# Local attention and SiLU MLP on one core: second MLP steps laid out behind a pair of first ones, and the q copy put ahead of the reciprocal on VectorE

## The chip, the core and the metric

The kernel runs on one core of a Trainium2 chip. The metric is the device time of one execution in microseconds (us), taken as the median of the runs; lower is better. The core has TensorE (PE, with its weight loads listed as PEld), VectorE (DVE), ScalarE (ACT), GpSimd (POOL) and SyncE (SP), which work through their own instruction streams and wait for one another through semaphores.

## What is computed

The inputs are q, k and v of shape 8 x 8 x 576 x 64 (batch, heads, positions, width) and two weights of 512 x 2048 and 2048 x 512. All are float32. Cut to what matters:

```python
# attention, per batch and head; S = 576, D = 64, factor = 4
q_d, k_d, v_d = means of q, k, v over groups of 4 positions        # 144 positions
out_d   = softmax(q_d @ k_d.T / 8) @ v_d                            # then repeated 4 times
out_loc = softmax(where(|i - j| < 4, q @ k.T / 8, -1e9)) @ v        # a band of 7 positions
x = (repeat(out_d, 4) + out_loc), heads side by side                # 4608 tokens x 512
# MLP
h = x @ w_in                                                        # 4608 x 2048
out = (h * sigmoid(h)) @ w_out                                      # 4608 x 512
```

## The kernel before

The attention goes by pairs of heads: pair p (0 to 31) holds heads 2p and 2p+1, and four pairs make one batch element, that is 576 tokens of x and all its 512 columns (column block kc is pair 4b+kc). The MLP goes by blocks j (0 to 8) of 512 tokens. x is kept transposed in `xT`, a ring of 1536 tokens, so block j can start only when the pairs that make its tokens are done: block 2 needs pair 11, block 3 pair 15, block 4 pair 19, block 5 pair 23, block 6 pair 27, blocks 7 and 8 pair 31.

The work is written as units. A unit is a few instructions on one engine, with a name. The names used below, for pair p:

- On PE: `T` transposes q into PSUM bank `o0` and k into bank `pe_`; `S` makes the scores in bank pair `AB`; `Z` makes the sums of exponentials and `PV` the weighted values, both in `CD`; `VP` makes v's group sums (up to pair 13 only); `RB` spreads the reciprocals over the partitions (up to pair 9 only). From n = 10 on, one unit `V`n holds S of pair n, T of pair n+1, PV of pair n-2 and Z of pair n-1, in this order of instructions. `g1_j_f` is a first MLP step: four matmuls (kc = 0 to 3) that make 128 columns (f of 16) of h for block j, in one of the two banks of `HP`. `g2_j_tt_part` is a quarter of a second MLP step: four matmuls of the product of 128 tokens (tt of 4) with w_out, into bank `o0` (from the 23rd step on alternately `pe_` and `o0`).
- On VectorE: `eq` copies the transposed q out of `o0` (ScalarE does it for pairs below 12); `mk` and `mq` make the group sums of k and q; `r` is the reciprocal of the sums in `CD`; `m` multiplies `CD` by the spread reciprocals `Rb` into `xo`; `k` masks the exponentials; `s` is the second half of SiLU on one g1.
- On ScalarE: `ek` copies k out of `pe_`; `x` and `xd` are the exponentials; `t` is the tanh of one g1 (so a bank of `HP` is free after g1, t and s); `o` copies a finished g2 out of its bank. From pair 10 on its queue also issues `z`, which writes the reciprocals to DRAM, and two `b`, which read them back spread over the partitions into `Rb`.
- On GpSimd: `c` and `cw` cast q/k and v; `va` and `vb` make v's group sums from pair 14 on out of the load `vq`; `a` adds the two attention results into `xT`.
- SP's queue issues the loads (`lq`, `lk`, four `lv`, three `lvq` per pair, released by the exponential of an earlier pair) and the `out` stores.

The order on each engine is not written out. The program creates the units in one sequence, and `Plan.order` then lays them out by list scheduling: with the costs written in the code it takes, on the engine that can go first, the ready unit with the lowest priority number among the next few (14 on PE, 40 on ScalarE and VectorE). A unit's number is its place in the sequence unless `prio` gives another; `t` and `s` have -1, `o` has -3, `r` has -400000, `z` and `b` have -500000. A dictionary `FIRST` can hold a written-out order for an engine's first units; in the kernel before it is empty. The order so found is then run in that order by each engine, with waits only where data or buffers ask for them.

The sequence from n = 10 on is one loop: V, then RB, VP and new loads where there are any, then four g1 and one g2 in its four parts, mixed. When the pairs are done, the loop goes on with g1 and g2 alone.

Of the kernel before, what the change touches and what calls it, by code (L numbers as in the profile page):

```python
# [15 lines left out]
NPAIR = B_ * H_ // 2  # L16
# [145 lines left out]


FIRST = {
}

class Plan:
# [109 lines left out]
def bass_hourglass_attn__then__act_silu_kernel(  # L277
# [9 lines left out]
    with kctx:  # L287
        E = kctx.enter_context
        L = Plan()
        res = {}  # L290

        def R(name, psum=False):
            if name not in res:
                res[name] = Res(name, psum)
            return res[name]

        def sb(name, shape, dt, n=1):
            ts = [E(nc.sbuf_tensor(f"{name}{i}", shape, dt)) for i in range(n)]
            return ts if n > 1 else ts[0]
# [22 lines left out]
        zr = sb("zr", [128, 72], F32, 2)  # L322
# [30 lines left out]
        def one(eng, name, cost, fn, r=(), w=(), dma=None, prio=None, dcost=0.0):  # L353
            u = L.unit(eng, name, cost, prio, dcost)
            L.op(u, fn, r, w, dma)
            return u
# [4 lines left out]
        def copy(eng, e, out_, in_):  # L361
            return e.activation(out_, in_, AF.Copy) if eng == "ACT" else e.tensor_copy(out_, in_)
# [3 lines left out]
        def half(j):  # L366
            return slice(64 * j, 64 * j + 64)
# [95 lines left out]
        def dma(eng, name, out_, in_, w, sem, dcost, r=(), prio=None, cost=0.42):  # L463
            return one(eng, name, cost, lambda s: s.dma_start(out_, in_), r, w, sem, prio, dcost)  # L464
# [98 lines left out]

        def pe_T(u, p):
            a, b = p % NB, (p - 1) % NB
            for r in range(9):
                for j, h, x, t, n in ((0, 0, 0, o0, a), (0, 1, 1, pe_, a), (1, 1, 0, o0, a), (1, 0, 1, pe_, b)):
                    o = t[half(h), 0:288].bitcast(BF16)[:, 64 * r:64 * r + 64]  # L570
                    w = qkb[n][half(j), x, 64 * r:64 * r + 64]
                    L.op(u, lambda e, o=o, w=w, j=j: e.transpose(o, w, idn[half(j), :]),  # L572
                         [R("id"), R(f"qkb{n}{x}")], [rE if x else rF])

        def after_T(p):
            j = p % NT
            eng = "ACT" if p < NEQ else "DVE"
            one(eng, f"eq{p}", 0.68 if p < NEQ else 0.72, lambda e: copy(
                eng, e, qT[j][:, :].rearrange("p (g r) -> p g r", r=9),
                o0[:, 0:288].bitcast(BF16).rearrange("p (r g) -> p g r", r=9)),  # L580
                r=[rF], w=[R(f"qT{j}")])
            one("ACT", f"ek{p}", 0.68, lambda e: e.activation(  # L582
                kT[j][:, 3:579].rearrange("p (g r) -> p g r", r=9),
                pe_[:, 0:288].bitcast(BF16).rearrange("p (r g) -> p g r", r=9), AF.Copy),
                r=[rE], w=[R(f"kT{j}")])
            one("DVE", f"mk{p}", 0.74, lambda e: e.tensor_reduce(  # L586
                kd[j][:, 0:SD], kT[j][:, 3:579].rearrange("p (g r) -> p g r", r=4), AX.X, ALU.add),
                r=[R(f"kT{j}")], w=[R(f"kd{j}")])
            if p >= NMQ:
                one("DVE", f"mq{p}", 0.74, lambda e: e.tensor_reduce(  # L590
                    qd[j][:, :], qT[j][:, :].rearrange("p (g r) -> p g r", r=4), AX.X, ALU.add),
                    r=[R(f"qT{j}")], w=[R(f"qd{j}")])
                return
            half_ = vt[:, :, :].rearrange("p a b -> p (a b)")[:, 0:288].rearrange("p (g r) -> p g r", r=2)
            q4 = qT[j][:, :].rearrange("p (g r) -> p g r", r=4)
            u = L.unit("POOL", f"mq{p}", 1.2)
            L.op(u, lambda g: g.tensor_tensor(half_, q4[:, :, 0:2], q4[:, :, 2:4], ALU.add),
                 r=[R(f"qT{j}")], w=[R("vt")])
            L.op(u, lambda g: g.tensor_tensor(qd[j][:, :].unsqueeze(2), half_[:, :, 0:1], half_[:, :, 1:2], ALU.add),
                 r=[R("vt")], w=[R(f"qd{j}")])  # L600
# [49 lines left out]
        def acc(p):  # L650
            return (HP, rH) if p < 4 and p % 2 else (CD_, rCD_)
# [48 lines left out]
        def after_Z(p):  # L700
            i, u = p % 2, p % NR
            CD, rCD = acc(p)
            if p < NDIR:
                (h, m, l), rp = [rpart[p % 2][:, k, :] for k in range(3)], rpr[p % 2]
                zs, rest, rz = zr[i][:, :], rrest[p % 2][:, :], R(f"rrest{p % 2}")
                sg = [R("sgn0"), R("sgn1")]
                one("DVE", f"r{p}", 0.56, lambda e: e.reciprocal(zs, CD[:, 0, 360:432]), r=rCD[:1], w=[R(f"zr{i}")],  # L707
                    prio=-400000)
                one("ACT", f"rh{p}", 0.25, lambda e: e.activation(h, zs, AF.Copy), r=[R(f"zr{i}")], w=[rp[0]],
                    prio=-400000)  # L710
                one("DVE", f"rx{p}", 0.2, lambda e: e.scalar_tensor_tensor(  # L711
                    rest, h, sgn[:, 0:1], zs, ALU.mult, ALU.add), r=[R(f"zr{i}"), rp[0]] + sg, w=[rz], prio=-400000)
                one("DVE", f"rm{p}", 0.15, lambda e: e.tensor_copy(m, rest), r=[rz], w=[rp[1]], prio=-400000)
                one("DVE", f"rl{p}", 0.2, lambda e: e.scalar_tensor_tensor(  # L714
                    l, m, sgn[:, 1:2], rest, ALU.mult, ALU.add), r=[rz, rp[1]] + sg, w=[rp[2]], prio=-400000)
                return
            one("DVE", f"r{p}", 0.56, lambda e: e.reciprocal(zr[i][:, :], CD[:, 0, 360:432]),
                r=rCD[:1], w=[R(f"zr{i}")], prio=-400000)
            eng = "ACT"
            dma(eng, f"z{p}", scr[u][0:74, :], zr[i][0:74, :], [R(f"scr{u}")], f"scr{u}", 0.2, r=[R(f"zr{i}")], prio=-500000)  # L720
            for h in range(2):
                src = bass.AP(tensor=scr[u].tensor, offset=scr[u].offset + 64 * h * 72, ap=[[0, 64], [1, 720]])
                dma(eng, f"b{p}", Rb[u][half(h), :], src, [R(f"Rb{u}{h}")], f"Rb{u}{h}", 0.85,
                    r=[R(f"scr{u}")], prio=-500000)
# [49 lines left out]
        def g1(j, f):  # L774
            n = ng1[0]
            ng1[0] += 1
            hb, tb = n % 2, n % 2
            t0 = (512 * j) % XR
            u = L.unit("PE", f"g1_{j}_{f}", 0.934)
            for kc in range(4):  # L780
                mm(u, hps[hb], w_in_sb[:, kc, 128 * f:128 * f + 128], xT[:, kc, t0:t0 + 512].bitcast(F32R),
                   [R(f"w_in{f // 4}")] + xblk(kc, 512 * j, 512 * j + 512), [rH[hb]], start=(kc == 0), stop=(kc == 3))
            one("ACT", f"t{j}_{f}", 0.62, lambda e: e.activation(th[tb][:, :], hps[hb], AF.Tanh, scale=0.5),  # L783
                r=[rH[hb]], w=[R(f"th{tb}")], prio=-1)
            one("DVE", f"s{j}_{f}", 0.71, lambda e: e.scalar_tensor_tensor(  # L785
                gT[j % 2][:, f, :], th[tb][:, :], 1.0, hps[hb], ALU.add, ALU.mult),
                r=[rH[hb], R(f"th{tb}")], w=[R(f"g{j % 2}_{f}")], prio=-1)
# [19 lines left out]
        def T(p):  # L807
            made.add(("T", p))
            u = L.unit("PE", f"T{p}", 0.45 if p > 1 else 0.9)
            pe_T(u, p)  # L810
            after_T(p)

        def VP(p):
            u = L.unit("PE", f"VP{p}", 0.4 if p > 1 else 0.8)
            pe_VP(u, p)
            after_VP(p)
# [69 lines left out]
        def G1(n):  # L886
            for _ in range(n):
                if todo:
                    g1(*todo.pop(0))

        def G2(parts):
            j, tt = todo2[0]
            u = 4 * j + tt
            bank, rb = (o0, rF) if u < 22 or u % 2 else (pe_, rE)
            for p in parts:
                g2(j, tt, p, bank, rb)
            if parts[-1] == 3:
                todo2.pop(0)
# [20 lines left out]
        while todo or todo2:  # L919
            if n < NPAIR + 2:  # L920
                V(n)
                if n <= NDIR:
                    RB(n - 1)
                if n <= NVP:
                    VP(n - 1)
                feed()
            G1(1)
            G2((0,))
            G1(1)
            G2((1,))  # L930
            G1(1)
            G2((2, 3))
            G1(1)
            n += 1
        P = Prog()
        for u in L.order({"PE": 14, "ACT": 40, "DVE": 40, "POOL": 30, "SP": 40}, FIRST):
            plan_log.append((u.start, u.cost, u.eng, u.name))
# [35 lines left out]
```

The softmax here doesn't subtract the row's maximum and nothing guards it: scores larger than these inputs give would overflow.

## Time and profile before

| what | value |
|---|---|
| median of 3 runs | 357.08 us (356.82 to 357.63) |
| the profiled execution | 357.98 us, its span 356.2 us |
| mean granted TensorE clock | 0.986 |
| one g1, in a row of eight matmuls | 0.92 us |
| one g2 of 16 matmuls | 3.45 to 3.47 us |
| reciprocal (r), q copy (eq) on VectorE | 0.61 us, 0.70 us |
| m, k, mk, mq, s on VectorE | 0.90, 0.45, 0.73, 0.74, 0.69 us |
| tanh (t), copy of a g2 (o) on ScalarE | 0.60 us, 0.60 us |
| loads into vq, Rb: from issue to landing (median) | 5.2 us, 4.2 us |

The times of single instructions come from the one profiled execution, whose span of 356.2 us is 1.8 us less than its own time. The profile's rows show start, duration, engine, line, operation and `out<-in` by the program's names without buffer numbers, and, in square brackets, how long the engine had been idle and what ended that. A line such as L359 or L464 belongs to a helper that issues every matmul or every DMA, so rows are told apart by tile: `HP` is g1, `o<-w_out_bf` is g2, `AB` is S or RB, `CD` is PV and Z, `o<-idn` and `pe_<-idn` are T.

### The profile page before, as it was taken

The numbers are of one execution on the slowest core, as the hardware profiler recorded it, in microseconds if no ns is written. First come the engines' busy times: TensorE is split into PE (matmuls) and PEld (weight loads), VectorE is DVE, ScalarE is ACT, GpSimd is POOL, SyncE is SP. The second block draws the span as 40 slices with busy tenths as digits, with TensorE's granted clock in tenths as the row PEclk, the third lists the DMA queues.
The fourth block names the chain that finished last, engine by engine and source line by source line (L and its number), as shares of the span: only waits on it lengthen the run. The fifth ranks groups of instructions, "written<-read, shape, count | busy, mean of one in ns | idle before, by whom it ended". The sixth has DMA issues, their size and how long they took to land.

```text
span 356.2 us, 11025 instructions
## 1 busy us (share of the span) xinstructions
PE 327.2 (92%) x4742; PEld 212.7 (60%) x4742; DVE 228.1 (64%) x392; ACT 181.8 (51%) x326; POOL 156.8 (44%) x203
## 2 busy tenths in 40 slices
PE   1574599899999999999999999999999999999996
PEld 0453477666666666666666665666665666666642
DVE  7589889876667777777776766677754434343400
ACT  2766478766554555555555554555543343434321
POOL 7977874272374675664667367555111100000000
PEclk9998689999999999999999999999999999999999
DMA  8999999946878877778887987873222000110012
GB/s 230 248 264 243 302 297 219 220 131 179 235 193 237 223 225 223 221 201 226 233 227 193 229 240 206 194 182 107 65 111 77 31 29 29 51 39 29 31 59 88
DMA packets 73506, 60.28 MB, mean 169 GB/s; under 512 B 47986, under 2 KB 55794, under 8 KB 73458
## 3 DMA queue, kind: packets, MB, share of 16 engines
q1 hardware_dynamic: 63818, 44.27, 47.5%
q10 hardware_dynamic: 5416, 9.02, 8.7%
q0 software_dynamic: 4224, 6.29, 7.5%
q8 instruction: 37, 0.61, 0.7%
q14 instruction: 11, 0.09, 0.1%
HBM read 51.76 MB, written 9.91 MB: 173 GB/s over the span
## 4 chain that ended last, share of the span: by engine, by line
PE 79%; DVE 7%; DMA 4%; SPq 4%; ACT 3%; issue 2%; POOL 1%; POOLq 0%; ACTq 0%; DVEq 0%
PE HP L359 35%; PE o L359 25%; PE pe_ L359 8%; PE CD L359 5%; SPq L464 4%; PE AB L359 3%; DMA vq<-in_v_dram 3%; PE o L572 1%; DVE rrest L711 1%; DVE rp L714 1%; DMA vs<-in_v_dram 1%; DVE Pt L628 1%; DVE xo L745 1%; DVE zr L707 1%; DVE gT L785 1%
## 5 line engine op out<-in xcount | busy, mean ns | idle before, releaser
L785 DVE SCALAR_TENSOR_TENSOR gT<-th,HP 128x512 bf16<-128x512 f32 x144 | 96.6, 684 | 101.2 <-ACT th L783 100.8
L359 PE MATMUL HP<-xT,w_in_sb 128*128 128x512 f32 x576 | 160.0, 416 | 1.6 <-DVE gT L785 0.7
L783 ACT ACTIVATE th<-HP 128x512 f32<-128x512 f32 x144 | 86.2, 599 | 75.3 <-PE HP L359 73.4
L359 PEld LDWEIGHTS HP<-xT,w_in_sb 128*128 128x128 f32 x576 | 106.0, 189 | 28.9 <-DVE gT L785 1.3
L359 PE MATMUL o<-w_out_bf,gT 128*128 128x512 bf16 x464 | 107.0, 380 | 0.0
L359 PEld LDWEIGHTS o<-w_out_bf,gT 128*128 128x128 bf16 x464 | 42.6, 98 | 54.3 <-issue 8.6
L769 POOL TENSOR_TENSOR xT<-xo 128x576 fp32r<-128x576 f32 (+3 forms) x48 | 42.9, 907 | 44.5 <-DVE xo L745 44.5
L800 ACT ACTIVATE osb<-o 128x512 f32<-128x512 f32 x29 | 17.4, 599 | 60.4 <-PE o L359 60.3
L559 POOL TENSOR_TENSOR vt<-vq 128x512 f32<-128x512 f32 x18 | 23.0, 1278 | 56.0 <-DMA vq<-in_v_dram 55.9
L544 POOL CAST qkb<-qk 128x1152 bf16<-128x1152 f32 x30 | 36.8, 1226 | 6.9 <-PE pe_ L572 4.7
L745 DVE TENSOR_TENSOR xo<-CD,Rb 128x720 f32<-128x720 f32 x30 | 27.0, 899 | 1.0 <-ACT Rb L735 0.6
L554 POOL CAST vb<-vs 128x640 bf16<-128x640 f32 x30 | 22.1, 736 | 11.3 <-PE CD L359 5.6
L572 PE MATMUL o<-idn,qkb 64*64 64x64 bf16 x576 | 17.4, 202 | 9.9 <-DVE qkb L539 6.3
L359 PE MATMUL pe_<-w_out_bf,gT 128*128 128x512 bf16 x112 | 26.4, 380 | 0.0
L586 DVE TENSOR_REDUCE kd<-kT 128x144 bf16<-128x576 bf16 x32 | 23.3, 731 | 0.9 <-ACT kT L582 0.8
L582 ACT ACTIVATE kT<-pe_ 128x576 bf16<-128x576 bf16 x32 | 21.0, 655 | 1.9
L628 DVE TENSOR_TENSOR Pt<-Pt,mask_bf 128x576 bf16<-128x576 bf16 x32 | 20.7, 647 | 0.8 <-ACT Pt L624 0.8
L624 ACT ACTIVATE Pt<-AB 128x576 bf16<-128x576 f32 x32 | 20.7, 646 | 0.6 <-PE AB L359 0.4
L572 PEld LDWEIGHTS o<-idn,qkb 64*64 64x64 bf16 x576 | 13.9, 117 | 9.7 <-DVE qkb L539 6.3
L572 PE MATMUL pe_<-idn,qkb 64*64 64x64 bf16 x576 | 16.3, 202 | 2.0 <-DVE qkb L541 1.0
L359 PEld LDWEIGHTS pe_<-w_out_bf,gT 128*128 128x128 bf16 x112 | 10.0, 98 | 13.6 <-issue 3.2
L590 DVE TENSOR_REDUCE qd<-qT 128x144 bf16<-128x576 bf16 x24 | 17.8, 742 | 0.0
(79 smaller groups left out, 311.9 us busy)
## 6 DMA issues: line engine op xcount, KB each, us to landing
vs<-in_v_dram SPq DMA_DIRECT2D x126, 80.0 KB, 4.2
qk<-in_q_dram SPq DMA_DIRECT2D x32, 288.0 KB, 3.6
out_dram<-osb SPq DMA_DIRECT2D x36, 256.0 KB, 3.3
qk<-in_k_dram SPq DMA_DIRECT2D x30, 288.0 KB, 4.8
Rb<-scr ACTq DMA_DIRECT2D x44, 180.0 KB, 4.2
vq<-in_v_dram SPq DMA_DIRECT2D x18, 256.0 KB, 5.2
w_in_sb<-in_moe_w_in_dram POOLq DMA_DIRECT2D x4, 1024.0 KB, 10.6
w_out_bf<-in_moe_w_out_dram POOLq DMA_DIRECT2D x4, 512.0 KB, 11.2
```

The source lines that it names most:

```text
L359: L.op(u, lambda t: t.matmul(out_, lhsT, rhs, start=start, stop=stop, skip_group_check=True), r, w)
L544: one("POOL", f"c{p}", 1.15, lambda g: g.tensor_copy(qkb[j][:, :, :], qk[i][:, :, :]), r=[R(f"qk{i}0"), R(f"qk{i}1")], w=[R(f"qkb{j}0"), R ...
L554: one("POOL", f"cw{p}", 0.72, lambda g: g.tensor_copy(vb[m][:, :, :], vs[i][:, :, :]), r=rr, w=[R(f"vb{m}")])
L559: one("POOL", f"va{p}", 1.3, lambda g: g.tensor_tensor(vt[:, :, :], vq[i][:, :, 0:128], vq[i][:, :, 128:256], ALU.add), r=rr, w=[R("vt")])
L572: L.op(u, lambda e, o=o, w=w, j=j: e.transpose(o, w, idn[half(j), :]), [R("id"), R(f"qkb{n}{x}")], [rE if x else rF])
L582: one("ACT", f"ek{p}", 0.68, lambda e: e.activation(kT[j][:, 3:579].rearrange("p (g r) -> p g r", r=9), pe_[:, 0:288].bitcast(BF16).rearra ...
L586: one("DVE", f"mk{p}", 0.74, lambda e: e.tensor_reduce(kd[j][:, 0:SD], kT[j][:, 3:579].rearrange("p (g r) -> p g r", r=4), AX.X, ALU.add), ...
L628: one("DVE", f"k{p}", 0.46, lambda e: e.tensor_tensor(Pt[m][:, :, :], Pt[m][:, :, :], mask_bf[:, :].unsqueeze(1).to_broadcast([128, 2, 288 ...
L745: one("DVE", f"m{p}", 0.92, prio=-450000 if L.boost else None, r=rCD + [R(f"Rb{u}0"), R(f"Rb{u}1")], w=[R(f"xo{x}")], fn=lambda e: e.tenso ...
L769: one("POOL", f"a{p}", 0.15 + n * 0.0019, lambda g, dst=dst, in0=in0, in1=in1: g.tensor_tensor(dst, in0, in1, ALU.add), r=[R(f"xo{x}")], w ...
L783: one("ACT", f"t{j}_{f}", 0.62, lambda e: e.activation(th[tb][:, :], hps[hb], AF.Tanh, scale=0.5), r=[rH[hb]], w=[R(f"th{tb}")], prio=-1)
L785: one("DVE", f"s{j}_{f}", 0.71, lambda e: e.scalar_tensor_tensor(gT[j % 2][:, f, :], th[tb][:, :], 1.0, hps[hb], ALU.add, ALU.mult), r=[rH ...
```

## The change

It has three parts.

1. `FIRST` is filled: the order of the first units is written out for all five engines, up to the unit RB9 on PE, ev9 on ScalarE, mq11 on VectorE, the last piece of a8 on GpSimd, and the first DMA of lv13 on SP. From there on the planner goes by its rule again.
2. `eqi` records the place of each pair's `eq` unit. The reciprocal of pair p (p of 10 and more) no longer has priority -400000, but the place of eq of pair p+2 plus a half; both belong to the same V step. For pairs 30 and 31, which have no such eq, it is the unit's own place.
3. In the loop, the four g1 and the g2 are created in another sequence: part 0 of g2, two g1, parts 1 to 3, two g1.

```diff
 FIRST = {
+    "PE": """
+        T0 T1 S0 T2 S1 Z0 VP0 T3 Z1 RB0 PV0 VP1 S2 T4 PV1 RB1 Z2 VP2 S3 T5 PV2 Z3 RB2 VP3 S4 T6 PV3 RB3 Z4
...
+        g1_0_14 RB8 g1_0_15 g1_1_0 g1_1_1 V10 g1_1_2 g1_1_3 VP9 g2_0_0_0 g2_0_0_1 g2_0_0_2 RB9""",
...
 }
...
+        eqi = {}
+
...
             eng = "ACT" if p < NEQ else "DVE"
+            eqi[p] = len(L.units)
             one(eng, f"eq{p}", 0.68 if p < NEQ else 0.72, lambda e: copy(
...
             one("DVE", f"r{p}", 0.56, lambda e: e.reciprocal(zr[i][:, :], CD[:, 0, 360:432]),
-                r=rCD[:1], w=[R(f"zr{i}")], prio=-400000)
+                r=rCD[:1], w=[R(f"zr{i}")], prio=eqi[p + 2] + 0.5 if p + 2 < NPAIR else None)
...
                 feed()
-            G1(1)
             G2((0,))
-            G1(1)
-            G2((1,))
-            G1(1)
-            G2((2, 3))
-            G1(1)
+            G1(2)
+            G2((1, 2, 3))
+            G1(2)
             n += 1
```

More of the change, by code (lines that the diff above doesn't have):

```diff
@@ L164 @@
 FIRST = {
+    "PE": """
+        T0 T1 S0 T2 S1 Z0 VP0 T3 Z1 RB0 PV0 VP1 S2 T4 PV1 RB1 Z2 VP2 S3 T5 PV2 Z3 RB2 VP3 S4 T6 PV3 RB3 Z4
+        VP4 S5 T7 Z5 RB4 VP5 PV4 g1_0_0 g1_0_1 S6 T8 g1_0_2 g1_0_3 RB5 Z6 g1_0_4 S7 g1_0_5 PV5 VP6 g1_0_6
+        RB6 T9 Z7 g1_0_7 g1_0_8 S8 PV6 VP7 g1_0_9 g1_0_10 RB7 T10 Z8 g1_0_11 g1_0_12 S9 PV7 VP8 g1_0_13
+        g1_0_14 RB8 g1_0_15 g1_1_0 g1_1_1 V10 g1_1_2 g1_1_3 VP9 g2_0_0_0 g2_0_0_1 g2_0_0_2 RB9""",
+    "ACT": """
+        lkx lk0 ckx eq0 ek0 cw0 eq1 ek1 cw1 x0 xd0 eq2 ek2 x1 xd1 ev0 rh0 eq3 ek3 eb0 rh1 ev1 x2 xd2 eq4 ek4
+        eb1 rh2 ev2 x3 xd3 eq5 ek5 eb2 rh3 ev3 x4 xd4 eq6 ek6 eb3 rh4 ev4 x5 xd5 eq7 ek7 eb4 rh5 ev5 t0_0
+        t0_1 x6 xd6 eq8 t0_2 t0_3 eb5 ek8 rh6 t0_4 x7 xd7 t0_5 ev6 t0_6 eb6 eq9 ek9 rh7 t0_7 t0_8 x8 xd8 ev7
+        t0_9 t0_10 eb7 eq10 ek10 rh8 t0_11 t0_12 x9 xd9 ev8 t0_13 t0_14 eb8 t0_15 t1_0 t1_1 eq11 ek11 rh9
+        t1_2 t1_3 x10 xd10 ev9""",
@@ new lines @@
+    "DVE": """
+        const const.1 const.2 const.3 const.4 const.5 const.6 const.7 const.8 const.9 const.11 const.10
+        const.12 const.14 const.13 const.15 const.16 const.17 const.18 const.19 const.20 const.21 const.22
+        const.23 zero const.24 const.25 const.37 const.38 const.39 const.40 const.41 const.67 const.70
+        const.68 const.71 cq0 const.26 const.27 cq1 ck0 ck1 const.62 const.63 const.64 const.65 mk0 mk1 k0
+        mk2 r0 k1 rx0 rm0 rl0 r1 mk3 m0 rx1 rm1 rl1 k2 r2 mk4 rx2 m1 rm2 k3 rl2 r3 mk5 m2 rx3 rm3 rl3 k4 r4
+        mk6 rx4 m3 rm4 k5 rl4 r5 mk7 rx5 m4 rm5 rl5 s0_0 s0_1 k6 mq8 s0_2 r6 s0_3 mk8 rx6 s0_4 rm6 k7 rl6 m5
+        s0_5 s0_6 r7 mq9 mk9 rx7 s0_7 rm7 s0_8 rl7 k8 m6 s0_9 s0_10 r8 mq10 mk10 rx8 s0_11 rm8 s0_12 rl8 k9
+        m7 s0_13 s0_14 s0_15 s1_0 s1_1 r9 m8 mk11 rx9 s1_2 rm9 s1_3 rl9 mq11""",
@@ new lines @@
+    "POOL": """
+        const.28 const.31 const.29 const.32 const.30 const.33 const.34 const.35 const.36 const.66 const.69
+        const.42 const.43 const.44 const.45 const.46 const.47 const.48 const.49 const.50 const.51 const.52
+        const.53 const.54 const.55 const.56 const.57 const.58 const.59 const.60 const.61 mq0 c2 mq1 c3 mq2
+        cw2 c4 w0 cw3 mq3 c5 a0 cw4 mq4 w1 c6 a1 cw5 mq5 a2 w2 c7 cw6 mq6 a3 c8 cw7 w3 a4 mq7 c9 cw8 w4 c10
+        w5 a5 w6 cw9 w7 a6 a7 c11 cw10 c12 cw11 cw12 c13 a8 a8.1 a8.2""",
@@ L165 @@
+    "SP": """
+        lq0 lq1 lk1 lv0.1 lv0.2 lv0.3 lq2 lv0e lv0 lk2 lv1 lv1.1 lv1.2 lv1.3 lq3 lk3 lv2 lv2.1 lv2.2 lv2.3
+        lq4 lk4 lv3 lv3.1 lv3.2 lv3.3 lq5 lk5 lv4 lv4.1 lv4.2 lv4.3 lq6 lk6 lv5 lv5.1 lv5.2 lv5.3 lq7 lk7
+        lv6 lv6.1 lv6.2 lv6.3 lq8 lk8 lv7 lv7.1 lv7.2 lv7.3 lq9 lk9 lv8 lv8.1 lv8.2 lv8.3 lq10 lk10 lv9
+        lv9.1 lv9.2 lv9.3 lq11 lk11 lv10 lv10.1 lv10.2 lv10.3 lv11 lv11.1 lv11.2 lv11.3 lq12 lk12 lq13 lk13
+        lv12 lv12.1 lv12.2 lv12.3 lq14 lk14 lv13""",
 }
```

## The prediction

> **What bounds the kernel now.** I read the page's busy times and its 40 slices first.
>
> ```profile
> PE 327.2 (92%) x4742; PEld 212.7 (60%) x4742; DVE 228.1 (64%) x392; ACT 181.8 (51%) x326; POOL 156.8 (44%) x203
> PE   1574599899999999999999999999999999999996
> ```
>
> TensorE (PE) is the limit from about 46 us on. The table of stages (PE, PEld, DVE, ACT, POOL busy; clock; DMA share; GB/s) says how completely:
>
> ```profile
> 46.00:78.00 32.00, 30.12 (x595) 22.42 (x594) 27.17 (x50) 23.82 (x46) 17.03 (x20) 0.99 1.09 226
> 145.00:187.00 42.00, 42.00 (x686) 27.17 (x686) 32.43 (x50) 21.92 (x39) 24.97 (x26) 1.00 0.79 222
> 187.00:216.00 29.00, 28.33 (x509) 18.43 (x507) 20.09 (x33) 15.44 (x28) 17.22 (x23) 1.00 0.85 226
> 216.00:248.00 32.00, 32.00 (x471) 20.49 (x458) 24.56 (x39) 16.62 (x29) 18.96 (x19) 1.00 0.67 171
> 275.00:339.00 64.00, 64.00 (x287) 39.11 (x285) 25.27 (x37) 26.35 (x44) 1.22 (x1) 1.00 0.10 36
> ```
>
> Pair 10 begins the part that the change reaches (V11 ends at 85 us). From there PE is idle in one place only, 0.67 us between 187 and 216. A busy PE can still hide a stall, so I measured the rhythm too: each reciprocal of L717 starts as its V step ends, so the distance of two of them is one period. VectorE's timeline gives
>
> ```profile
> 103.43 0.61 DVE L717 RECIPROCAL zr<-CD 128x72 f32<-128x72 f32 x1
> 111.56 0.61 DVE L717 RECIPROCAL zr<-CD 128x72 f32<-128x72 f32 x1
> ...
> 120.59 0.61 DVE L717 RECIPROCAL zr<-CD 128x72 f32<-128x72 f32 x1
> 121.11 0.70 DVE L362 COPY qT<-o 128x576 bf16<-128x576 bf16 x1
> ...
> 129.21 0.61 DVE L717 RECIPROCAL zr<-CD 128x72 f32<-128x72 f32 x1
> ...
> 206.93 0.61 DVE L717 RECIPROCAL zr<-CD 128x72 f32<-128x72 f32 x1
> ...
> 216.53 0.61 DVE L717 RECIPROCAL zr<-CD 128x72 f32<-128x72 f32 x1
> ```
>
> A plain period is 8.62 us (120.59 to 129.21): V, two g1, four g2, two g1. Periods with a VP step are 9.04. Three others are short because they hold three g1, not four (8.13 with a VP from V13 to V14; 7.70 from V21 to V22, made up by 9.55 with five after it; 7.74 from V29 to V30). Only V25 to V26 is long without return: 216.53 - 206.93 = 9.60, a loss of about 0.97 us. PE's timeline shows its cause:
>
> ```profile
> 212.11 1.97 PE L359 MATMUL HP<-xT,w_in_sb 128*128 128x512 f32 x7
> 214.75 0.50 PE L359 MATMUL HP<-xT,w_in_sb 128*128 128x512 f32 x1 [0.67 <-POOL xT L769]
> ```
>
> The last of eight matmuls, g1_5_0's with kc=3, waits for a23. POOL has a23 queued behind va27, cw27, vb27 and c28, and va27 waited 3.17 us for its vq load. In the kernel before, g1_5_0 stands ahead of V26, so V26 waits with it.
>
> **The skill.** "PSUM — Partial Sum Buffer", section "PSUM bank collisions raise a hardware error", has a PSUM bank guarded as a whole against two engines. The trace agrees: T's first transposes into o0 start after the ACT copy has left it (copy 109.44 to 110.04, T at 110.47). The same page, "Engine vs sequencer instructions", calls the ScalarE and VectorE queues strict FIFO; agreeing, a tanh ready at about 126.7 waits at 127.36 behind two b issues. "VectorE: DVE Perf Modes", section "The DRAIN you can't avoid", says that an instruction waits until the pipe is empty: here the copy starts 0.52 after a reciprocal of 0.61, so the records overlap by 0.09, and swapping the two leaves their sum as it is.
>
> **Part 1, FIRST.** I compared these five lists with the order that the kernel before lays out: all are its first 82 (PE), 100 (ACT), 141 (DVE), 81 (POOL) and 83 (SP) names, without a difference. Nothing before V11 moves: cost 0.
>
> **Part 2, eq ahead of r, 20 pairs.** No instruction is added. eq (0.70) starts 0.52 earlier, r (0.61) some 0.7 later. What would gain is g2, which needs bank o0 from eq. But eq ends at 121.11 + 0.70 = 121.81 and g2 starts at 122.46, when the two g1 ahead of it are through: 0.65 us of slack already, so the gain is 0. What could lose is r's chain. z goes out behind a tanh, about 1.1 us later (121.23 to 122.34). It has a row of cover: the b loads of that pair are issued at 126.21, and z needs 2.9 us (112.20 to 115.16, where b waits for nothing else). In about half of the periods b now stands ahead of the o copy at r + 3.5 (132.70 for r15); I expect it behind o in all, at r + 5.6 as for r14. Rb then lands at about r + 5.6 + 0.55 + 4.2 (the page's median) = 10.4; m starts at r + 12.3 (132.85 for r14), and would start about 0.4 later, because tanh outputs now overtake mq on VectorE. Slack 1.9 or more, 0 even at the longest landing (6.2). Cost taken: 0; bounds: -0.1 to +0.1 per period at most if landing stays in its range. The mq and k that finish some 0.4 later are used 3 us later or more. Behind the b issues a first tanh starts 0.3 later, which V covers (V15's period has this order and lasts 8.62).
>
> **Part 3, the loop.** The planner takes, of ready units, the lowest number; V is numbered ahead of its group. I followed its rule by hand with the costs written in the code, for the order alone and not for times. In most groups both programs give V, g1, g1, g2 x4, g1, g1: G2((0,)) is first by number, but waits for eq. The two groups where a g1 cut into a g2 (V22, V30) become whole; PE was full there, gain 0. In the tail the third g1 isn't ready after one g2, so it stays two g1, two g2: 3.58 us a round at full PE before and after, gain 0. What changes is which of V and a new block's first g1 comes first, through the earlier o copy (b no longer ahead of it):
> - V13/V14. Block 1's sixteen g1 are used up two groups early. Before, g1_2_0 stood between g2_0_3_3 and V14. Now V14's bank comes free by the planner's figures some 0.2 us ahead of a11, so V14 follows the g2 directly. Its S part (0.27) runs, but T15 waits for the o0_3 copy, which ends at 110.04. T starts at about 110.08, and T to the end of V takes 111.48 - 110.47 = 1.01: end at 111.09. Before, V14 ended at 111.48 with g1_2_0 (0.92) done. Loss 111.09 + 0.92 - 111.48 = 0.53. Bounds: 0 if g1_2_0 still goes first, 0.83 if S's start has the gap of 0.28 that follows a g1 and T does not catch up.
> - After that groups and blocks are aligned: four g1 of one block per group, and a new block's first g1 always behind V18, V22, V26 and V30. At V25/V26 two g1 of block 4 fill the time of the o copy; V26 starts without a wait at about 214.2, and g1_5_0 follows at 215.5, when a23's first piece (214.18 + 0.5) is there. Gain 0.97. Bounds: 0.67 (the idle shown) to 0.97.
>
> Nothing is added to SP's or POOL's queues; out DMAs and loads keep their order, the `a` steps stay behind the casts they stand behind now.
>
> **Sum.** -0.97 + 0.53 = -0.44 us. Profiled execution: 357.98 (span 356.2, 1.8 us around it), which gives 357.54; that execution lies 0.90 above the median, and the difference carried to the median of 357.08 gives 356.64: I say 356.6. A difference under 0.2% (0.71 us) can't be told from none.
>
> **Rivals.**
> - A, the forecast, aligned with one bare V14: 356.6. Chance 0.50. For it: one stall in the whole of pairs 11 to 31, which the new order avoids; against it: the choice at V14 turns on 0.2 us of the planner's figures.
> - B, no bare V14 (g1_2_0 still first, the phase put right at V18): 357.08 - 0.97 = 356.1. Chance 0.22. No larger gain is in sight, since PE is otherwise full at the full clock (1.00).
> - C, nothing: the order stays as it was at V25, or a wait of the same size moves elsewhere: 357.1. Chance 0.08.
> - D, slower: bare V steps recur. If the blocks run out early at the later boundaries too (V17/18, V21/22, V29/30), T waits for its o copy at each, 0.53 a time: four make 2.12 - 0.97 = +1.15, so 358.2. Two of them cancel the gain; it is slower by 0.2% from four on (1.68 / 0.53 = 3.2). For it: before, four of the five block boundaries (all but V17/18) disturb the rhythm. Against it: once aligned, two g1 are always left. Chance 0.12.
> - E, slower too: b behind o collides with vq loads, and Rb lands after m. m has 1.9 us, and the k and g1 products behind it on VectorE another 2, so landing must go from 4.2 to beyond 8; each microsecond past that costs one in each of 19 periods. One would give 376, a tenth 359. Chance 0.08; the longest landing seen is 6.2.
>
> **Numbers.** Likeliest 356.6. Range 355.8 to 358.3: B with 0.3 for run to run at the low end, D at the high end; A's own range is 356.1 (gain 0.97, no loss) to 357.2 (gain 0.67, loss 0.83). Faster by over 0.2% (under 356.37): B and a tail of A, 0.27. Slower: D and E with a small part of C, 0.20. Within: 0.53.
>
> **What would show it.** Reciprocal-to-reciprocal times: V25 to V26 at 8.6 (9.6 would refute the gain); a PE wait on ACT osb in front of transposes near 109.6, and a V13-to-V14 distance near 7.7; the qT copy 0.5 ahead of the reciprocal in every period with g2's start unmoved; b issues behind the osb copies throughout; xo (m) without a wait on a DMA; tail rounds of 3.58. A repeated idle of PE with o<-osb as its releaser means D; VectorE waiting for DMA Rb means E.

## The result and the profile after

| kernel | median | range, runs | ratio to the kernel before, 95% interval | profiled execution, span |
|---|---|---|---|---|
| before | 357.29 us | 355.2 to 359.35, 20 | 1 | 357.98 us, 356.2 us |
| after | 359.05 us | 356.68 to 360.61, 20 | 1.0046 [1.0027, 1.0065] | 358.24 us, 356.5 us |

The change makes the kernel slower by 0.46%. The prediction had 356.6 us, a small gain, with a range of 355.8 to 358.3.

The page of the profiled execution after it, busy times and the 40 slices of PE:

```profile
PE 332.7 (93%) x4742; PEld 218.0 (61%) x4742; DVE 222.5 (62%) x392; ACT 180.2 (51%) x326; POOL 156.3 (44%) x203
...
PE   1685699999999999999999999999999999999996
```

PE is busy 5.5 us longer with the same 4742 matmuls; 3.9 us of that lie in the first 46 us (26.63 against 22.71), which the change leaves as they were. The next rows are from the table of stages: start and end, length, busy time of PE, PEld, DVE, ACT and POOL, then clock, DMA share and GB/s. They show the stall's stage and the stretch from V10 to V30 in after, and then V10 to V30 in before:

```profile
187.00:216.00 29.00, 29.00 (x526) 19.29 (x525) 19.98 (x33) 15.45 (x28) 16.62 (x22) 1.00 0.78 216
...
73.92:249.28 175.36, 174.99 (x2798) 114.17 (x2797) 123.59 (x200) 92.24 (x166) 100.35 (x113) 1.00 0.71 201
```

```profile
74.65:248.80 174.15, 173.48 (x2798) 112.85 (x2797) 126.79 (x200) 93.79 (x166) 101.10 (x113) 1.00 0.75 204
```

The idle 0.67 us between 187 and 216 is gone, as forecast. But from V10 to V30 PE is busy 1.51 us longer for the same number of matmuls, at full clock. Idle time can't explain that; the rhythm has to be looked at. VectorE's timeline of after, the reciprocals:

```profile
146.52 0.60 DVE L752 RECIPROCAL zr<-CD 128x72 f32<-128x72 f32 x1
155.29 0.60 DVE L752 RECIPROCAL zr<-CD 128x72 f32<-128x72 f32 x1
...
207.79 0.60 DVE L752 RECIPROCAL zr<-CD 128x72 f32<-128x72 f32 x1
216.56 0.60 DVE L752 RECIPROCAL zr<-CD 128x72 f32<-128x72 f32 x1
```

V25 to V26 has come down from 9.60 to 8.77. But a plain period, such as 146.52 to 155.29, is now 8.77 as well, where it was 8.62 to 8.66. PE's timeline of after says where in the period this is: V19 and the MLP step behind it, then the same V step of before.

```profile
153.03 0.35 PE L391 MATMUL AB<-qT,kT 64*64 64x58 bf16 x20
...
153.62 0.46 PE L391 MATMUL CD<-Pt,vb 64*64 64x58 bf16 x20
...
154.43 0.73 PE L391 MATMUL HP<-xT,w_in_sb 128*128 128x512 f32 x2
```

```profile
153.78 0.35 PE L359 MATMUL AB<-qT,kT 64*64 64x58 bf16 x20
...
154.37 0.34 PE L359 MATMUL CD<-Pt,vb 64*64 64x58 bf16 x20
...
155.06 0.74 PE L359 MATMUL HP<-xT,w_in_sb 128*128 128x512 f32 x2
```

From its first row to the first HP row, V takes 154.43 - 153.03 = 1.40 us after and 1.28 before. The 20 small matmuls of PV (`CD<-Pt,vb`) take 0.46 in place of 0.34: between two of them PE starts nothing for 0.09 us. No wait is shown there, and the gap counts as busy time: the record of one such matmul lasts about 0.19 us, so the one ahead covers the gap. This is so in all fourteen V steps from V17 to V30 (1.38 to 1.41, together 19.51 us against 17.84), and in none from V10 to V16. ScalarE's timeline shows what lies beside it; after first, then before:

```profile
151.35 0.60 ACT L835 ACTIVATE osb<-o 128x512 f32<-128x512 f32 x1 [2.93 <-PE o L391]
152.22 0.60 ACT L818 ACTIVATE th<-HP 128x512 f32<-128x512 f32 x1 [0.27 <-PE HP L391]
152.23 1.12 ACTq L496 DMA_DIRECT2D Rb<-scr  x2
153.39 0.60 ACT L818 ACTIVATE th<-HP 128x512 f32<-128x512 f32 x1 [0.57 <-PE HP L391]
```

```profile
152.10 0.60 ACT L800 ACTIVATE osb<-o 128x512 f32<-128x512 f32 x1 [2.51 <-PE o L359]
152.13 1.10 ACTq L464 DMA_DIRECT2D Rb<-scr  x2
153.28 1.21 ACT L783 ACTIVATE th<-HP 128x512 f32<-128x512 f32 x2 [0.57 <-PE HP L359]
```

After, the order is o, tanh, two b, tanh. The second b issue ends at 152.23 + 1.12 = 153.35, that is 0.32 us after V's start, and the second tanh waits for it. Before, b was ahead of both tanh (or ahead of o), and over before V began.

From the start of V10 to the start of V30 it is 175.37 us after and 174.15 before: +1.22. That is made of the stall removed at V26 (-0.97), a V14 that is 0.56 longer, and the fourteen longer V steps, +1.66 together; sum +1.25. Against the median of before this is a ratio of 1.0034, within the measured interval. (In the two profiled executions V10 itself starts 0.73 us apart, 73.92 and 74.65, in a stretch where all orders are the same; so the spans hide the difference, and I compare stages. These are the figures of one execution of each kernel; the ratios come from all runs.)

### The profile page after: what moved, and what is told of

Its sections match the earlier page's. It is cut to its first block, busy times and chain, and to the rows that moved or that the text cites. A ratio compares the mean times of both kernels' runs of the same rounds, so it can differ in the third digit from the quotient of the medians.

```text
span 356.5 us, 11028 instructions
## 1 busy us (share of the span) xinstructions
PE 332.7 (93%) x4742; PEld 218.0 (61%) x4742; DVE 222.5 (62%) x392; ACT 180.2 (51%) x326; POOL 156.3 (44%) x203
## 4 chain that ended last, share of the span: by engine, by line
PE 87%; DVE 7%; ACT 2%; POOL 2%; issue 1%; DVEq 0%; ACTq 0%
PE HP L391 38%; PE o L391 28%; PE pe_ L391 8%; PE CD L391 6%; PE AB L391 4%; POOL xo L414 2%; PE o L606 2%; DVE rrest L746 1%; DVE xo L780 1%; DVE rp L749 1%; DVE gT L820 1%; DVE Pt L663 1%; DVE kd L621 1%; PE pe_ L606 1%; ACT Rb L770 0%
## 5 line engine op out<-in xcount | busy, mean ns | idle before, releaser
L820 DVE SCALAR_TENSOR_TENSOR gT<-th,HP 128x512 bf16<-128x512 f32 x144 | 98.0, 683 | 102.0 <-ACT th L818 101.7
L391 PE MATMUL HP<-xT,w_in_sb 128*128 128x512 f32 x576 | 158.1, 415 | 0.8 <-DVE gT L820 0.7
L804 POOL TENSOR_TENSOR xT<-xo 128x576 fp32r<-128x576 f32 (+3 forms) x48 | 44.5, 939 | 60.2 <-DVE xo L780 60.2
L576 POOL CAST qkb<-qk 128x1152 bf16<-128x1152 f32 x30 | 34.7, 1155 | 7.3 <-PE pe_ L606 5.0
L663 DVE TENSOR_TENSOR Pt<-Pt,mask_bf 128x576 bf16<-128x576 bf16 x32 | 16.7, 521 | 0.5 <-ACT Pt L659 0.5
```

The source lines that it names most:

```text
L391: L.op(u, lambda t: t.matmul(out_, lhsT, rhs, start=start, stop=stop, skip_group_check=True), r, w)
L576: one("POOL", f"c{p}", 1.15, lambda g: g.tensor_copy(qkb[j][:, :, :], qk[i][:, :, :]), r=[R(f"qk{i}0"), R(f"qk{i}1")], w=[R(f"qkb{j}0"), R ...
L804: one("POOL", f"a{p}", 0.15 + n * 0.0019, lambda g, dst=dst, in0=in0, in1=in1: g.tensor_tensor(dst, in0, in1, ALU.add), r=[R(f"xo{x}")], w ...
```

## The experiments

**What stretches V: ScalarE's order, VectorE's order or PE's groups?** Four kernels, timed together. The first two have every order written out and differ from after and from before in ScalarE's list alone.

x1_b_ahead, after with b ahead of both tanh (one of fourteen places):

```diff
-        x17 t2_12 xd17 z16 t2_13 o1_3 t2_14 b16 b16.1 t2_15 ek19
+        x17 t2_12 xd17 z16 t2_13 o1_3 b16 b16.1 t2_14 t2_15 ek19
```

> The changed kernel with the order of every engine written out as it was, but on ScalarE, from V17 to V30, both b DMA issues stand directly behind the o copy, ahead of the two tanh (o b b t t in place of o t b b t). Theory (a b issue between the two tanh falls into the V step and stretches it): all V steps from V17 on go back from about 1.40 to about 1.27 us, each plain period from 8.75 to about 8.63, together about 1.7 us less than the changed kernel: ratio to the kernel before about 0.999 (a gain of 0.4 us). Rival (the swap of eq and r on VectorE, or the way TensorE's groups lie, stretches V): V steps stay at 1.40 and the ratio stays near 1.0035 to 1.0045.

x2_b_between, before with b between the tanh:

```diff
-        x17 z16 t2_13 t2_14 xd17 b16 b16.1 o1_3 t2_15 t3_0 ek19
+        x17 z16 t2_13 t2_14 xd17 o1_3 t2_15 b16 b16.1 t3_0 ek19
```

> The kernel before with the order of every engine written out as it was, but on ScalarE, from V17 to V30, the two b DMA issues are put between the two tanh that follow o (o t b b t). Nothing of the change is in it. Theory (b between the tanh stretches V): 12 to 14 V steps go from 1.27 to about 1.40 us, 1.4 to 1.7 us in all, ratio about 1.004 to 1.005. Rival (VectorE's order or TensorE's groups do it): V steps stay at 1.27, ratio 1.000.

p2_eq_first and p3_loop are the two parts of the change by themselves, with the planner free:

```diff
 # p2_eq_first: after, with the loop of before
-            G2((0,))
-            G1(2)
-            G2((1, 2, 3))
-            G1(2)
+            G1(1)
+            G2((0,))
+            G1(1)
+            G2((1,))
+            G1(1)
+            G2((2, 3))
+            G1(1)
 # p3_loop: after, with the priority of before
-                r=rCD[:1], w=[R(f"zr{i}")], prio=eqi[p + 2] + 0.5 if p + 2 < NPAIR else None)
+                r=rCD[:1], w=[R(f"zr{i}")], prio=-400000)
```

> The changed kernel with the old loop (G1, G2 (0), G1, G2 (1), G1, G2 (2, 3), G1): eq ahead of r alone. Laid out, it has a bare V14 (no first MLP step ahead of it), no first step that waits for a23, and b between two tanh from V16 on. Theory: +0.53 at V14, -0.97 at V26 and about 14 times +0.12 in the V steps, +1.3 us, ratio about 1.0035, like the changed kernel. Rival (the new loop makes the loss): the V steps are 1.27 long and the ratio is about 0.999.

> The changed kernel with r ahead of eq as in the kernel before: the new loop alone. Laid out, V14 keeps a first MLP step ahead of it, V26 has none that waits for a23, and both b stand ahead of the o copy or of both tanh, never between two tanh. Theory: V steps of 1.27, V25 to V26 at 8.6, no loss at V14: -0.97 us, ratio about 0.9973. Rival (the new loop's own grouping stretches V): V steps of 1.40 from V17 on, ratio about 1.002.

| kernel | ratio, 95% interval | V17 to V30, summed | V10 to V30 |
|---|---|---|---|
| x1_b_ahead | 1.0010 [0.9981, 1.0039] | 19.00 us | 174.83 us |
| x2_b_between | 1.0056 [1.0030, 1.0081] | 19.49 us | 175.11 us |
| p2_eq_first | 1.0065 [1.0037, 1.0092] | 19.31 us | 175.61 us |
| p3_loop | 0.9994 [0.9968, 1.0021] | 17.86 us | 174.40 us |

The interval of x1 covers what both theories expect, so the lengths of the V steps decide. The cause is ScalarE's order. x2 has nothing of the change in it but the place of b, and its PE timeline shows V19 as after has it:

```profile
152.15 0.35 PE L458 MATMUL AB<-qT,kT 64*64 64x58 bf16 x20
...
152.74 0.45 PE L458 MATMUL CD<-Pt,vb 64*64 64x58 bf16 x20
...
153.53 0.74 PE L458 MATMUL HP<-xT,w_in_sb 128*128 128x512 f32 x2
```

x2 shows one thing more. It keeps the order of before, with g1_5_0 ahead of V26, and yet its PE has no wait for a23 there: V26 starts as the two g1 ahead of it are through, and V25 to V26 takes 213.47 - 204.71 = 8.76, a plain stretched period.

```profile
204.71 0.35 PE L458 MATMUL AB<-qT,kT 64*64 64x58 bf16 x20
...
211.34 2.20 PE L458 MATMUL HP<-xT,w_in_sb 128*128 128x512 f32 x8
213.47 0.35 PE L458 MATMUL AB<-qT,kT 64*64 64x58 bf16 x20
```

In x2 va27, which POOL does ahead of a23, had its load and could start at 206.44, 1.73 after V25's start; in before that was 4.68 after V25's start (210.26). So the 0.97 of the stall is what the profiled execution of before lost; how many of its executions lose it isn't shown.

In x1 twelve of the fourteen V steps are back at 1.27 or 1.28 and one is 1.32. The miss is V19, 2.38 long: x1's rows of ScalarE and PE there are

```profile
152.46 1.10 ACTq L563 DMA_DIRECT2D Rb<-scr  x2
153.61 1.09 ACT L885 ACTIVATE th<-HP 128x512 f32<-128x512 f32 x2 [2.08 <-PE pe_ L673]
```

```profile
154.98 1.19 PE L458 MATMUL HP<-xT,w_in_sb 128*128 128x512 f32 x4 [0.93 <-DVE gT L887]
```

Here b waited for the reciprocals to be written by z (issued at 146.93, 5.5 us before b, where 2.9 had been seen), with both tanh behind it, so PE ran out of free HP banks for 0.93 us. p3 shows nothing of its expected -0.97 (174.40 us from V10 to V30, against 174.15 before), in part for a like reason: its V steps are 1.27 to 1.28 but for V16 (1.77), where the two b issues took 2.00 us in place of 1.10, ahead of both tanh. Besides, PE waited for xT just ahead of V14 and of V18, 0.4 us in all, and the two periods are 0.43 and 0.50 longer than before. The Trainium skill ("Perfetto Trace Analysis", section "DMA Instruction — HWDGE (DVE, Sync)") counts into an issue's duration the wait for the descriptor block that the issuing engines share; this agrees with it, as b's second issue took 1.51 us while a vq issue of SyncE beside it took 1.52, and the two ended 0.02 us apart. So b ahead of the tanh is no cure: it trades 0.12 us in each V step for a rarer stall, 1.11 us in x1 and 0.50 in p3. p2 confirms that part 2 alone brings the long V steps, and the long V14 (1.83) as well. Its ratio is above the expected 1.0035 and above what its stages give (175.61 - 174.15 = 1.46 us, 1.0041); the rest wasn't traced.

**The late tanh, or the issue itself?** After has both in the same place. Three kernels part them; the fourth adds a repair of V14.

x3_late_tanh delays the second tanh without b, x4_b_on_sp keeps b there without delaying the tanh, x6_b_behind puts b behind both tanh:

```diff
 # x3_late_tanh, on x1_b_ahead: one more activation, du, per pair 15 to 28
-        o1_3 b16 b16.1 t2_14 t2_15 ek19
+        o1_3 b16 b16.1 t2_14 du16 t2_15 ek19
 # x4_b_on_sp, on after: ScalarE's list without b15 to b28, SyncE's with them
-        lvq20.2 out1_3 lq22
+        lvq20.2 b16 b16.1 out1_3 lq22
 # x6_b_behind, on after
-        o1_3 t2_14 b16 b16.1 t2_15 ek19
+        o1_3 t2_14 t2_15 b16 b16.1 ek19
 # x8_best, on x6_b_behind: PE, ScalarE, VectorE
-        g2_0_3_3 V14 g1_2_0 g1_2_1 VP13
+        g2_0_3_3 g1_2_0 V14 g1_2_1 VP13
-        o0_3 b12 b12.1 ek15 x14 t2_0
+        o0_3 t2_0 b12 b12.1 ek15 x14
-        k13 eq15 r13 mk15 mq15 s2_0
+        k13 s2_0 eq15 r13 mk15 mq15
```

> As x1_b_ahead, with one more ScalarE activation (a copy of 128x192 of a constant to a tile that nothing reads) between the two tanh of V17 to V30, so that the second tanh starts about 0.35 to 0.40 us after V's start, as in the changed kernel, while both b issues are over before V. Theory L (what stretches V is the late second tanh itself): V steps of 1.38 to 1.41 from V17 on, ratio about 1.004. Theory B (it is a b issue that ends inside V, about 0.3 us before TensorE's gap): V steps of 1.27, and about the time of x1_b_ahead.

> The changed kernel, but the 28 b DMAs of pairs 15 to 28 are issued by SyncE, just ahead of the out DMA that goes out around the start of the same V step, in place of ScalarE; no tanh stands behind them. Theory S (only an issue on ScalarE's own queue matters): V steps of 1.27 from V17 on. Theory D (any issue of these 64-row DMAs that ends inside V stretches it, whichever engine issues): V steps of 1.35 to 1.40 wherever SyncE's b ends between 0.2 and 0.4 us after V's start, and 1.27 elsewhere.

> The changed kernel with both b issues of V17 to V30 behind both tanh (o t t b b): they are then issued inside V, between about 0.1 and 1.3 us after its start, and the kT copy waits for them. No tanh is late. If a b issue in V is enough to stretch it: V steps of 1.38 or more, no gain. If it takes a b issue that holds up the second tanh: V steps of 1.27, about 1.7 us less than the changed kernel, ratio about 0.999; the only two V steps of this kind seen so far (V14 of the changed kernel, V19 of p2_eq_first) show no gap, so I expect the second.

> As x6_b_behind, and the first MLP step g1_2_0 (with its tanh and its product) is put ahead of V14, so that V14 no longer waits for the o copy. Expected: V14 of 1.27 in place of 1.83, 0.5 us less than x6_b_behind; with V steps of 1.27 the ratio is about 0.9975. If b behind the tanh still stretches V: about 1.002.

| kernel | ratio, 95% interval | V17 to V30, summed | V10 to V30 |
|---|---|---|---|
| x3_late_tanh | 1.0024 [1.0000, 1.0048] | 18.83 us | 175.56 us |
| x4_b_on_sp | 1.0021 [0.9996, 1.0045] | 18.96 us | 176.30 us |
| x6_b_behind | 0.9985 [0.9955, 1.0015] | 17.85 us | 173.88 us |
| x8_best | 0.9966 [0.9942, 0.9990] | 17.90 us | 173.41 us |

x3 missed its aim in most periods (its second tanh started at 0.24 after V's start, not 0.35), and from V10 to V30 it takes 0.73 us more than x1, mostly because b waited for z again, with three things behind it. But two of its own V steps speak against theory L, the late tanh. x3's ScalarE rows of V21 (PE starts it at 172.03; the row at 172.67 is its second tanh) and V24 (197.96; the row at 198.36 is its first), and PV's row in each:

```profile
170.78 1.10 ACTq L565 DMA_DIRECT2D Rb<-scr  x2
...
172.67 0.59 ACT L890 ACTIVATE th<-HP 128x512 f32<-128x512 f32 x1
...
197.22 1.10 ACTq L565 DMA_DIRECT2D Rb<-scr  x2
198.36 0.60 ACT L890 ACTIVATE th<-HP 128x512 f32<-128x512 f32 x1 [1.48 <-PE HP L460]
```

```profile
172.62 0.34 PE L460 MATMUL CD<-Pt,vb 64*64 64x58 bf16 x20
...
198.55 0.47 PE L460 MATMUL CD<-Pt,vb 64*64 64x58 bf16 x20
```

In V21 the second tanh is as late as 0.64 after V's start, b is over 0.15 before it, and PV takes 0.34. In V24 b ends 0.36 after V's start, and PV takes 0.47. A tanh at 0.64 might only be too late to matter, though. The other profiles settle that: in seven V steps ahead of which both b issues are over, the second tanh starts 0.28 to 0.44 after V's start, as in after, and PV takes 0.34 (x1's V17, V18, V24 and V29, p3's V24, x7's V15, x8's V15). x1's V18, where the second of the two tanh ends at 144.88 and so starts at 144.29, 0.31 after V:

```profile
142.62 1.13 ACTq L563 DMA_DIRECT2D Rb<-scr  x2
143.80 1.08 ACT L885 ACTIVATE th<-HP 128x512 f32<-128x512 f32 x2 [0.61 <-PE HP L458]
```

```profile
143.98 0.35 PE L458 MATMUL AB<-qT,kT 64*64 64x58 bf16 x20
...
144.57 0.34 PE L458 MATMUL CD<-Pt,vb 64*64 64x58 bf16 x20
```

Theory L falls. x4 says the same from the other side, and theory S (only ScalarE's own queue matters) falls with it. (Its 176.30 holds a V15 of 2.15, where b13, left on ScalarE, waited for z, and 0.39 more from V10 to V11.) In x4 b is SyncE's, no tanh is late (each second one starts 0.11 after V's start, from V17 on), and V is stretched or not by where b's issue ends. SyncE's rows of x4 for V19 (starts at 154.45) and V24 (198.22), and PV's:

```profile
153.67 1.11 SPq L563 DMA_DIRECT2D Rb<-scr  x2
...
197.66 1.11 SPq L563 DMA_DIRECT2D Rb<-scr  x2
```

```profile
155.04 0.47 PE L458 MATMUL CD<-Pt,vb 64*64 64x58 bf16 x20
...
198.81 0.34 PE L458 MATMUL CD<-Pt,vb 64*64 64x58 bf16 x20
```

End at 0.33 after V's start: 0.47. End at 0.55: 0.34. x6 then has both b issues inside V, and at no cost, since they end at 0.56 and 1.23. Its PE and ScalarE rows of V17:

```profile
135.43 0.35 PE L458 MATMUL AB<-qT,kT 64*64 64x58 bf16 x20
...
136.02 0.34 PE L458 MATMUL CD<-Pt,vb 64*64 64x58 bf16 x20
...
136.70 0.50 PE L458 MATMUL HP<-xT,w_in_sb 128*128 128x512 f32 x1
```

```profile
135.54 0.60 ACT L885 ACTIVATE th<-HP 128x512 f32<-128x512 f32 x1 [0.32 <-PE HP L458]
135.54 1.11 ACTq L563 DMA_DIRECT2D Rb<-scr  x2
```

x6 has no stall at V26 either and loses only at V14; its ratio isn't clear of 1. x8 mends V14 too: it takes 1.27 in place of 1.83. x8 is the only version whose ratio is clearly below 1: it beats before by 0.34%.

I then put the V steps of all twelve profiles together (V10 to V30 where V doesn't wait for the o copy), and measured how much later the first matmul behind `CD<-Pt,vb` starts than 0.86 us after V's start:

| where a b issue ends, us after V's start | V steps | delay, us |
|---|---|---|
| no b issue ends between -0.3 and 1.4 | 116 | 0 in all |
| -0.3 to 0 only | 8 | 0 in all |
| one at 0.08 to 0.14 | 5 | 0 to 0.04 |
| one at 0.23 to 0.48 | 82 | 0.09 to 0.16, median 0.12, in all |
| 0.5 and later only | 33 | 0 in 32, 0.05 in one |

In 30 V steps without such a b, another DMA's issue on SyncE (out or vq) ends at 0.18 to 0.48 (in 18 of them at 0.23 to 0.48): delay 0 in all. So it isn't any issue.

**Is it what b reads, or how much?** Single runs, since the V steps are the measure.

```diff
 # x5_other_source, on after
                 src = bass.AP(tensor=scr[u].tensor, offset=scr[u].offset + 64 * h * 72, ap=[[0, 64], [1, 720]])
+                if 15 <= p < 29:
+                    src = bass.AP(tensor=q.tensor, offset=q.offset + 64 * h * 720, ap=[[720, 64], [1, 720]])
 # x7_half_rows, on after
+                nb = 360 if 15 <= p < 29 else 720
-                src = bass.AP(tensor=scr[u].tensor, offset=scr[u].offset + 64 * h * 72, ap=[[0, 64], [1, 720]])
-                dma(eng, f"b{p}", Rb[u][half(h), :], src, [R(f"Rb{u}{h}")], f"Rb{u}{h}", 0.85,
+                src = bass.AP(tensor=scr[u].tensor, offset=scr[u].offset + 64 * h * 72, ap=[[0, 64], [1, nb]])
+                dma(eng, f"b{p}", Rb[u][half(h), 0:nb], src, [R(f"Rb{u}{h}")], f"Rb{u}{h}", 0.85,
```

> The changed kernel with b between the two tanh as it is, but from pair 15 to 28 each b reads 64 different rows of 2,880 bytes of the input q in place of 64 times the same row of the scratch buffer; the wait for the scratch buffer, the size and the target stay. The reciprocals of these pairs are so left out of the output. If the repeated reading of one row in memory is what TensorE's gap comes from: V steps of 1.27 from V17 on. If it is the issue as such: V steps of about 1.40 as in the changed kernel.

> The changed kernel with b between the two tanh as it is, but from pair 15 to 28 each b brings 64 rows of 1,440 bytes, half of the 2,880; the other half of the reciprocals' tile keeps older values. If the gap goes with the bytes that are moved: about 0.06 in place of 0.12 us per V step (1.33), or none. If it goes with the number of rows in one issue (64 as before): V steps of about 1.40.

Neither matters: V17 to V30 sum to 19.51 us in x5 and 19.59 in x7, against 19.51 in after. (Their single times, 360.22 and 361.37 us beside 357.33 for before, are of one run each and carry nothing.) The gap goes with the place in time of b's issue, not with the source, the repeated row or the bytes. Through what the issue of b, or what follows on it in the DMA engines, reaches PE's stream, and what sets it apart from an out or vq issue, was not found and stays open; the number of rows in one issue was not varied.

## Why the prediction was wrong

- **What bounds the kernel** was read rightly: PE, at full clock, one stall. That no larger gain was in sight held; that nothing could lengthen a full PE was silently assumed.
- **Part 1, cost 0**: right. V10 to V11 takes 9.34 us in both.
- **Part 2** is the failing step. That g2 gains nothing held. The cover of Rb was thinner than forecast: not none but two `m` wait for it, 0.47 and 1.26 us (the later one for a load that took 6.8 us to land, where 6.2 had been the longest), though with no wait of PE behind either. I had b behind o in every period; from V17 on it went one place further, between the two tanh. What failed is "Cost taken: 0; bounds: -0.1 to +0.1 per period", with its reason "Behind the b issues a first tanh starts 0.3 later, which V covers (V15's period has this order and lasts 8.62)". In that period both b stood ahead of both tanh, and their issue ended 0.55 us before the next V step. Between the two tanh it ends 0.3 after V's start, and each such V is 0.12 longer: 1.66 in fourteen periods, not 0. I had counted what waits for b and for the tanh, and taken V's 1.27 as fixed. My own bound of 0.1 over 20 periods, 2.0 us, would have put the slow end at 358.6; I didn't carry it into the range. (The tanh said to be ready at about 126.7 was misread: its g1 ends at about 127.0, so b held it up by 0.3 us, the figure that the forecast used.)
- **Part 3, V14**: right in place, cause and size. Forecast 0.53, measured 1.83 - 1.27 = 0.56. But it belongs to part 2, through the earlier o copy, and not to the loop: p2, with the old loop, has it, and p3, with the new loop alone, has a V14 of 1.27. PE's rows of after show T waiting for the o copy behind a V14 without a first MLP step ahead of it:

```profile
108.67 0.35 PE L391 MATMUL AB<-qT,kT 64*64 64x58 bf16 x20
108.85 0.27 PE L391 MATMUL AB<-qd,kd 64*64 64x144 bf16 x8
...
109.49 0.21 PE L606 MATMUL o<-idn,qkb 64*64 64x64 bf16 x1 [0.37 <-ACT osb L835]
```

- **Part 3, V25/V26**: right for the two profiled executions, -0.97. In x6 and x8, whose V steps are short again, the distance is 8.66 and 8.62, against 9.60 before. Either part alone takes the stall away (8.77 in p2, 8.63 in p3), and x2 hasn't got it even in the old order, so part of this agreement may be luck.
- **Tail and queues**: right. From V30's start to the end of the span it is 107.2 us after and 107.4 before.
- **Rivals**: none was it. D had the slower side at 358.2, but by bare V steps at later block boundaries, and there was only one, V14. With x6's order, which takes the lengthening of V away, the rest of the forecast comes near: V10 to V30 is 173.88 against 174.15, a gain of 0.27 where the sum said 0.44.

## What to carry to other kernels

When an edit reorders a queue, ask of each DMA issue that moves not only who waits for it, but what dense work of other engines it will now lie beside; a part that reads "full before and after" can still get longer. Measure such a part by its own length (start of the first row to the start of the next step), since here 1.7 us of pauses read as busy time. If a DMA's issue has slack, try it behind the work that PE waits for, not ahead of it: in x1's V19 it stood ahead, and one late landing held up everything behind it in the queue.

## What was not expected of the hardware

A b issue (64 rows into SBUF, mostly 0.45 to 0.62 us on ScalarE's or SyncE's queue) that ended 0.23 to 0.48 us after V's start made PE pause for about 0.1 us, mostly some 0.3 us after the issue's end, in 82 V steps of 82. Where the same issue ended before V, or at 0.5 and later, PV began and ran as ever in all but one case. The window puts the pause at PV's run of 20 small matmuls, which PE otherwise starts within 0.15 us. Whether an issue that ends at another time brings no pause, or one that other work hides, isn't shown.
